# Layer one's fifth mixing product made as seven smaller ones, with the sums, gates and splits around it moved

## The chip, the core and the metric

The kernel runs on one core of a Trainium2 chip. The core has five engines with a queue of instructions each: TensorE (PE; its weight loads are shown apart as PEld), VectorE (DVE), ScalarE (ACT), GpSimd (POOL) and SyncE (SP), which here only issues DMAs. Sixteen DMA engines move the data. The metric is the device time of one execution in microseconds (us), lower is better. The result is fp32; every product is made of three matmuls of rounded parts (high by high, high by low, low by high).

## What is computed

Four residual layers over x of 2048 × 512: a linear attention block and a gated MLP that mixes along the sequence, and both once more with the same weights. A pair of the two is called a layer here ("layer one", "layer two"; `L` 0 and 1).

```python
def _A_ref(x, wqkv, wo):                 # H = 32 heads of 16
    q, k, v = qkv[0], qkv[1], qkv[2]     # of x @ wqkv
    phi = lambda t: jnp.where(t > 0, t + 1, jnp.exp(t)) + 1e-6
    pq, pk = phi(q), phi(k)
    kv = jnp.einsum("bhsd,bhse->bhde", pk, v)
    z = jnp.einsum("bhsd->bhd", pk)
    num = jnp.einsum("bhqd,bhde->bhqe", pq, kv)
    den = jnp.einsum("bhqd,bhd->bhq", pq, z)[..., None] + 1e-6
    return (num / den).transpose(...).reshape(B, S, D) @ wo

def _B_ref(x, w_in, w_sp, b_sp, w_out):  # Fh = 896
    z = _gelu(jnp.einsum("bsd,df->bsf", x, w_in))
    z1 = z[..., :Fh]
    z2 = _layernorm(z[..., Fh:], axis=-1)
    g = jnp.einsum("ts,bsf->btf", w_sp, z2) + b_sp[None, :, None]
    return jnp.einsum("bsf,fd->bsd", z1 * g, w_out)

x = A_x
x = x + _A_ref(_layernorm(x, axis=-1), A_wqkv, A_wo)
x = x + _B_ref(_layernorm(x, axis=-1), B_w_in, B_w_sp, B_b_sp, B_w_out)
x = x + _A_ref(...)                      # the same weights again
x = x + _B_ref(...)
```

The product of `w_sp` (2048 × 2048) with `z2` (2048 × 896) is the mixing, and the largest part of the work.

## The kernel before

The order of the instructions on every engine is written out by hand in Python loops; nothing reorders them. Tiles come from lists of slots that are used round robin (`pages` 22, `quads` 6, `bigs` 4, `banks` 8, the last in PSUM). A tile that takes a slot waits for the last reader of the slot's former tile.

A layer runs through three classes. `P1.run` (the first half) takes the 16 row tiles of x one after another, one step `s` each: it normalises a tile, turns it (by a store to memory, tensor `xt`, a load and a transpose on VectorE, class `Turn`), makes K and Q and adds to the product of keys and values. Up to `s` = 10 a step holds 36 matmuls, then 24, since some Q are put off. `P2.run` (the second half) finishes the attention, and makes `z` and `z1`. `P4.run` is the mixing, and behind it the output products.

The mixing is a fast matrix product: with `w_sp` and `z2` cut in halves it takes seven products instead of eight. They come in the order P2, P1, P6, P7, P4, P5, P3. A product is eight steps `g`. In a step, `fetch` loads 512 KB of weights four steps ahead, `sp` splits them two steps ahead (ScalarE the high half, VectorE the low half, lines 885 and 886) together with the matching part of z2, and `mm` issues 24 or 18 matmuls (lines 1051 to 1053). At a product's end `evac` adds the banks to the result on VectorE. A finished unit of the result is multiplied by `z1` on POOL (`gate`, line 1089), one per step from the list `gq`; POOL's queue holds the gates in the order in which they are issued, and one starts as soon as its inputs are there.

A product whose name is in `DIVIDED` is itself made as seven smaller ones: 14 steps of 12 matmuls (`mm_div`, `evac_div`, `zsum`, `zpart`). In the kernel before, these are P2 and P4 of layer two and none of layer one.

Sums of parts of `w_sp` are needed by both forms. Those of the plain seven (`Sums.tick`, 32 ticks, tensor `s`) are added on POOL, 14 ticks in `P2.run` and the rest in the mixing of layer one (`g` up to 18). Those of the divided products (`Sums.halve`, 32 parts, tensor `hP`) are made by DMAs alone: first a copy issued by SP (line 791), then an accumulating DMA issued by POOL (line 795). They run from `g` = 19 on in layer one's mixing, beside P6, P7, P4, P5 and P3, and are read in layer two.

Of the kernel before, what the change touches and what calls it, by code (L numbers as in the profile page):

```python
# [15 lines left out]
P = 128  # L16
# [35 lines left out]

DIVIDED = ((), ("P2", "P4"))


@with_exitstack
def mixer_kernel(ctx: ExitStack, tc: tile.TileContext, x_in, wqkv, wo_d, win1_d, win2_d, wsp_d, bsp_d, wout_d,
# [156 lines left out]
    class Turn:  # L214
# [3 lines left out]
        def __init__(self, name, by_pe, always=False, inbank=False):  # L218
            self.name, self.by_pe, self.always, self.inbank = name, by_pe, always, inbank
            self.held, self.d, self.raw = {}, {}, {}  # L220

# [19 lines left out]
        def get(self, i):  # L241
            if i in self.held:
                s = self.held.pop(i)
                b = transposes(s)
                if self.always:
                    pages.put(s)
                return b, banks
            r = self.raw.pop(i)
            home = banks if self.inbank else pages
            y = home.get([P, 4, P])  # L250
            nc.vector.transpose(y.rearrange("p c (t m) -> p m c t", m=4), r.rearrange("p (m c j) -> p m c j", m=4, c=4))
            pages.put(r)
            return y, home


    class P1:
# [78 lines left out]
        def K_split(self, i):  # L335
            r = self.r.pop(i)
            h, l = pages.get(PAGE, F32R), pages.get(PAGE, F32R)
            nc.scalar.activation(h, r, AF.Copy, bias=PHI_EPS)
            last = nc.vector.scalar_tensor_tensor(l, r, PHI_EPS, h.bitcast(F32), op0=OP.add, op1=OP.subtract)
# [57 lines left out]
        def start(self):  # L397
# [14 lines left out]

            def idle(n):
                for _ in range(n):
                    nc.tensor.matmul(b, ones, m, start=True, stop=True)

# [5 lines left out]
            self.T_high(0)  # L422
            idle(4)
            banks.put(b)
# [117 lines left out]
    class P2:  # L542
# [121 lines left out]
        def e2(self, i):  # L664
            z = ztag(i, [P, FH], f"z{self.L}")
            for j, b in enumerate(self.eb):
                nc.scalar.activation(z[:, j * HF:(j + 1) * HF], b, AF.Gelu_apprx_tanh)
                banks.put(b)
# [26 lines left out]
        def run(self, sums):  # L695
            w1 = self.win1
            for s in range(1, NT + 3):
# [51 lines left out]
                w1.fetch()  # L749
                if self.L == 0 and s > 4:  # L750
                    sums.tick()
                if s >= NT + 1:
# [5 lines left out]
    class Sums:  # L758
# [70 lines left out]
    class P4:  # L829
# [8 lines left out]
        def __init__(self, p2, sums):  # L838
# [10 lines left out]
            self.tmp, self.bank = {}, {}  # L849
            self.beta = self.delta = None  # L850
            self.wout = {}
# [23 lines left out]
        def sp(self, g):  # L875
            self.wsp(g)
            if g < len(self.steps) and self.steps[g][0] not in self.div:
                self.zsp(g)

# [206 lines left out]
        def gate(self, n, f):  # L1086
            z1 = self.z1.pop((n, f))
            u = self.unit(n, f)
            nc.gpsimd.tensor_tensor(u, u, z1, op=OP.mult)  # L1089
            pages.put(z1)  # L1090

        def evac(self, p):

            V, bs = nc.vector, self.bs
            gates = []
            if p in ("P1", "P5"):
                for j in range(2):
                    n = 2 + j if p == "P1" else j
                    V.tensor_add(self.unit(n, 3), self.unit(n, 3) if self.joins(p) else bs[n],  # L1099
                                 self.delta[j])  # L1100
                    gates.append((n, 3))
                banks.put(*self.delta)
            for j in range(2):
                a, b = 2 + j, j
                for f in range(3):
# [21 lines left out]
                    if p in ("P2", "P4", "P3") or (p == "P7" and "P4" in self.div):  # L1127
                        banks.put(q)
            self.gq.extend(gates)

# [21 lines left out]
        def o(self, i):  # L1152
# [10 lines left out]
            if i % 4 == 3:  # L1163
                bigs.put(self.gb[i // 4])

        def run(self, nxt):
            p2 = self.p2
            self.fetch(2)
            self.sp(0)
            if self.div:  # L1170
                self.loadb()
            ahead = deque()
            if self.div:
                self.zpart(0)
                self.zpart(1)
                ahead.extend([2, 3, 4, 5, 6, 7][:4 - 2])
                self.zsum(2)
            while p2.f():
                if ahead:
                    g = ahead.popleft()  # L1180
                    self.zsum(g + 1)
                    self.zpart(g)
            while ahead:
                g = ahead.popleft()
                self.zsum(g + 1)
                self.zpart(g)
            p2.win1.free()
# [4 lines left out]
            for g in range(n):  # L1192
                p, k = self.steps[g]
                self.fetch(g + 4)
                evac_first = p == "P6" and k == HT - 1
                div_first = p in self.div and k == 13 and p == "P4"
                if not evac_first and not div_first:
                    self.sp(g + 2)
                    self.zsum(g + 4 + 1)
                    self.zpart(g + 4)  # L1200
# [21 lines left out]
                if p == "P3":  # L1222
# [85 lines left out]
```

## Time and profile before

| | us |
|---|---|
| median of three executions | 1387.16 |
| lowest and highest | 1387.02, 1388.31 |
| the profiled execution | 1386.75 |
| its span, first to last instruction | 1384.9 |

The mean granted clock of TensorE is 1.000. Rows of the order of time read: start in us, length in us, engine, line, operation, tile written <- tiles read, sizes, count, and in brackets the idle time of that engine before it and what ended it. A suffix q on an engine means its issuing queue. Rows of a window hold its ends, its length and the busy time of PE, PEld, DVE, ACT and POOL with their instructions, then the granted clock, the DMA engines' mean share and GB/s.

### The profile page before, as it was taken

The numbers are of one execution on the slowest core, as the hardware profiler recorded it, in microseconds if no ns is written. First come the engines' busy times: TensorE is split into PE (matmuls) and PEld (weight loads), VectorE is DVE, ScalarE is ACT, GpSimd is POOL, SyncE is SP. The second block draws the span as 40 slices with busy tenths as digits, with TensorE's granted clock in tenths as the row PEclk, the third lists the DMA queues.
The fourth block names the chain that finished last, engine by engine and source line by source line (L and its number), as shares of the span: only waits on it lengthen the run. The fifth ranks groups of instructions, "written<-read, shape, count | busy, mean of one in ns | idle before, by whom it ended". The sixth has DMA issues, their size and how long they took to land.

```text
span 1384.9 us, 17460 instructions
## 1 busy us (share of the span) xinstructions
PE 1376.4 (99%) x6182; PEld 1149.0 (83%) x6182; DVE 893.1 (64%) x1331; ACT 587.6 (42%) x893; POOL 396.7 (29%) x506
## 2 busy tenths in 40 slices
PE   9999999999999999999999999999999999999998
PEld 7888888888888888878888888888888888878887
DVE  6665877752578665674566658775438667886632
ACT  6664534434323333341256646443346333633410
POOL 3333455543466201342012334432100020021300
PEclk9999999999999999999999999999999999999999
DMA  5632267775999877893735322555346445454432
GB/s 159 202 115 62 92 213 258 250 240 193 329 309 317 302 248 190 228 266 114 228 112 185 115 61 95 175 179 168 114 148 202 137 167 155 147 186 149 161 123 91
DMA packets 148344, 248.76 MB, mean 180 GB/s; under 512 B 12448, under 2 KB 51104, under 8 KB 148000
## 3 DMA queue, kind: packets, MB, share of 16 engines
q1 hardware_dynamic: 145952, 239.26, 52.2%
q0 software_dynamic: 2304, 8.39, 3.4%
q8 instruction: 48, 0.79, 0.2%
q14 instruction: 40, 0.33, 0.1%
HBM read 179.70 MB, written 84.67 MB: 191 GB/s over the span
## 4 chain that ended last, share of the span: by engine, by line
PE 91%; DVE 4%; DMA 2%; ACT 2%; issue 1%; POOL 1%; SPq 0%; ACTq 0%; DVEq 0%; POOLq 0%
PE bank L125 18%; PE bank L124 18%; PE bank L123 18%; PE bank L1052 11%; PE bank L1053 11%; PE bank L1051 11%; DMA pg<-in_wout_dram 1%; DVE qd L886 1%; PE bank L515 1%; PE bank L526 0%; ACT qd L885 0%; DVE st L186 0%; PE bank L211 0%; DMA pg<-in_wqkv_dram 0%; DVE pg L112 0%
## 5 line engine op out<-in xcount | busy, mean ns | idle before, releaser
L1052 PE MATMUL bank<-qd,pg 128*128 128x512 f32 x784 | 305.5, 390 | 1.5 <-DVE qd L886 1.5
L1053 PE MATMUL bank<-qd,pg 128*128 128x512 f32 x784 | 305.3, 389 | 0.0
L1051 PE MATMUL bank<-qd,pg 128*128 128x512 f32 x784 | 305.1, 389 | 0.0
L886 DVE TENSOR_TENSOR qd<-qd,qd 128x1024 fp32r<-128x1024 f32 x124 | 166.7, 1345 | 135.3 <-ACT qd L885 135.0
L885 ACT ACTIVATE qd<-qd 128x1024 fp32r<-128x1024 f32 x124 | 131.3, 1059 | 184.4 <-PE bank L1053 158.9
L1052 PEld LDWEIGHTS bank<-qd,pg 128*128 128x128 f32 x784 | 147.1, 188 | 33.9 <-DVE qd L886 3.5
L1053 PEld LDWEIGHTS bank<-qd,pg 128*128 128x128 f32 x784 | 147.2, 188 | 31.1 <-DVE pg L925 0.7
L1051 PEld LDWEIGHTS bank<-qd,pg 128*128 128x128 f32 x784 | 147.1, 188 | 31.0 <-ACT pg L923 0.4
L1089 POOL TENSOR_TENSOR bg<-bg,pg 128x512 f32<-128x512 f32 x56 | 83.8, 1512 | 279.6 <-DVE bg L1099 121.0
L125 PE MATMUL bank<-qd,pg 128*128 128x512 f32 x384 | 149.8, 390 | 0.1
L190 POOL TENSOR_SCALAR rs<-mv 128x1 f32<-128x1 f32 x96 | 27.3, 284 | 343.5 <-DVE mv L188 342.8
L199 ACT ACTIVATE pg<-pg,nb,rs 128x512 f32<-128x512 f32 x63 | 51.2, 812 | 172.1 <-POOL nb L193 172.0
L123 PE MATMUL bank<-qd,pg 128*128 128x512 f32 x288 | 112.4, 390 | 0.1
L124 PE MATMUL bank<-qd,pg 128*128 128x512 f32 x288 | 112.2, 390 | 0.0
L805 POOL TENSOR_TENSOR pg<-pg,pg 128x512 f32<-128x512 f32 x64 | 93.8, 1466 | 55.0 <-DMA pg<-in_wsp_dram 46.0
L123 PE MATMUL bank<-bg,qd 128*128 128x448 f32 x256 | 94.2, 368 | 0.4 <-ACT qd L109 0.4
L125 PE MATMUL bank<-bg,qd 128*128 128x448 f32 x256 | 93.6, 365 | 0.1
L124 PE MATMUL bank<-bg,qd 128*128 128x448 f32 x256 | 93.6, 366 | 0.0
L125 PE MATMUL bank<-qd,bg 128*128 128x512 f32 x224 | 87.5, 391 | 0.0
L124 PE MATMUL bank<-qd,bg 128*128 128x512 f32 x224 | 87.4, 390 | 0.0
L123 PE MATMUL bank<-qd,bg 128*128 128x512 f32 x224 | 87.2, 389 | 0.0
L123 PE MATMUL bank<-wo,qd 128*128 128x512 f32 x224 | 87.1, 389 | 0.0
(137 smaller groups left out, 2557.9 us busy)
## 6 DMA issues: line engine op xcount, KB each, us to landing
qd<-s SPq DMA_DIRECT2D x64, 512.0 KB, 3.8
qd<-in_wsp_dram SPq DMA_DIRECT2D x44, 512.0 KB, 4.2
pg<-in_wsp_dram SPq DMA_DIRECT2D x64, 256.0 KB, 4.8
s<-pg SPq DMA_DIRECT2D x64, 256.0 KB, 4.5
pg<-x SPq DMA_DIRECT2D x64, 256.0 KB, 2.9
z<-pg SPq DMA_DIRECT2D x56, 256.0 KB, 2.8
pg<-z SPq DMA_DIRECT2D x56, 256.0 KB, 4.3
x<-pg SPq DMA_DIRECT2D x48, 256.0 KB, 2.6
```

The costliest lines, as they stand in the source:

```text
L123: nc.tensor.matmul(out, ah, bh, start=start, stop=False)
L124: nc.tensor.matmul(out, ah, bl, start=False, stop=False)
L125: nc.tensor.matmul(out, al, bh, start=False, stop=stop)
L190: nc.gpsimd.tensor_scalar(rs, mv[:, 1:2], LN_EPS, None, op0=OP.add)
L199: nc.scalar.activation(y, x, AF.Identity, bias=nb, scale=rs)
L805: nc.gpsimd.tensor_tensor(t, a, b, op=OP.add)
L885: self.mark = nc.scalar.activation(w[:, 0], r, AF.Copy)
L886: nc.vector.tensor_sub(w[:, 1], r, w[:, 0].bitcast(F32))
L1051: m(out, h[:, o], w[:, 0, j, :], start=start, stop=False, skip_group_check=True)
L1052: m(out, h[:, o], w[:, 1, j, :], start=False, stop=False, skip_group_check=True)
L1053: m(out, l[:, o], w[:, 0, j, :], start=False, stop=stop, skip_group_check=True)
L1089: nc.gpsimd.tensor_tensor(u, u, z1, op=OP.mult)
```

## The change

Layer one now divides P4. The 16 parts that this product's sums take are made in layer one's mixing at `g` = 10 to 25; those of layer two's P2 are made in layer two's `P1.run`, copies at `s` = 2 to 9 and accumulations at `s` = 6 to 13. Eight ticks of the plain sums move into layer one's `P1.run` (`s` = 2 to 9), into two slots of `bigs` cut in sheets. The loads of wv and wo move from `s` = 6 to 11 and 14. The transpose of a turned tile is issued at the end of the step before. A gate waits for the newest split of weights on ScalarE (`self.mark`). `evac` takes the two delta banks last, for layer one's P1 it is issued ahead of the next split, and at the end of P7 the split for P4's third step is issued ahead of the evacuation. Four warm-up matmuls at the start are 256 columns wide instead of 512.

```diff
-DIVIDED = ((), ("P2", "P4"))
+DIVIDED = (("P4",), ("P2", "P4"))
+
+class Sheets:
+    def __init__(self, slots, n):
+        self.slots = slots
+        self.tiles = [slots.get([P, NF, 512]) for _ in range(n)]
+        self.free_list = deque(t[:, f, :] for t in self.tiles for f in range(NF))
...
@@ Turn
+            self.pre(i)
+            return self.made.pop(i)
+
+        def pre(self, i):
+            if i in self.made or i not in self.raw:
+                return
             r = self.raw.pop(i)
...
-            return y, home
+            self.made[i] = y, home
...
@@ P1.start
-            idle(4)
+            idle(4, 256)
...
@@ P1.run
-                if s == 6:
-                    self.wv, self.wo = (quads.get([P, 4, 512]) for _ in range(2))
+                if self.L == 0:
+                    if s == 2:
+                        sums.slots = Sheets(bigs, 2)
+                    if 2 <= s < 10:
+                        sums.tick(s < 9)
+                    if s == 10:
+                        sums.store()
+                        sums.slots.close()
+                        sums.slots = pages
+                elif 2 <= s < 10:
+                    sums.halve(14 + s, None)
+                if self.L == 1 and 6 <= s < 14:
+                    sums.halve(18 + s, self.mark)
+                if s == 11:
+                    self.wv = quads.get([P, 4, 512])
                     nc.sync.dma_start(self.wv, wqkv[:, 1024:1536].rearrange("(c p) f -> p c f", p=P))
+                if s == 14:
+                    self.wo = quads.get([P, 4, 512])
                     nc.sync.dma_start(self.wo, wo_d.rearrange("(c p) f -> p c f", p=P))
+                if s in range(3,NT-1):
+                    self.turn.pre(s + 1)
...
@@ Sums
-            self.parts = [(what, p, m, q) for what in ("copy", "add") for p in DIVIDED[1] for m in (1, 3, 2, 4)
+            self.parts = [(what, p, m, q) for p in ("P4", "P2") for what in ("copy", "add") for m in (1, 3, 2, 4)
                           for q in range(2)]
...
@@ P4
-            nc.gpsimd.tensor_tensor(u, u, z1, op=OP.mult)
+            behind(nc.gpsimd.tensor_tensor(u, u, z1, op=OP.mult), self.mark)
...
+        def zahead(self, g):
+            while self.zmade <= g:
+                self.zsum(self.zmade + 1)
+                self.zpart(self.zmade)
+                self.zmade += 1
...
@@ P4.run
-                evac_first = p == "P6" and k == HT - 1
+                evac_first = (p == "P6" or p == "P1" and nxt is not None) and k == HT - 1
...
                 if evac_first:
+                    if p == "P1":
+                        self.ask(3)
                     self.evac(p)
                     self.sp(g + 2)
-                if g < 19:
-                    self.sums.tick()
-                if nxt is not None:
-                    self.sums.halve(g - 19, self.mark)
+                self.sums.tick()
+                if nxt is not None and 10 <= g < 26:
+                    self.sums.halve(g - 10, self.mark)
...
+                if p == "P7" and k == HT - 1 and self.div:
+                    self.sp(g + 3)
                 if k == HT - 1 and not evac_first:
                     self.evac(p)
```

More of the change, by code (lines that the diff above doesn't have):

```diff
@@ L338, in K_split @@
             nc.scalar.activation(h, r, AF.Copy, bias=PHI_EPS)
-            last = nc.vector.scalar_tensor_tensor(l, r, PHI_EPS, h.bitcast(F32), op0=OP.add, op1=OP.subtract)
+            last = self.mark = nc.vector.scalar_tensor_tensor(l, r, PHI_EPS, h.bitcast(F32), op0=OP.add,
+                                                              op1=OP.subtract)
             self.pk[i] = (h, l)
@@ L411, in start, with idle @@
             b = banks.get(PAGE)
-            def idle(n):
+            def idle(n, w=512):
                 for _ in range(n):
-                    nc.tensor.matmul(b, ones, m, start=True, stop=True)
+                    nc.tensor.matmul(b[:, 0:w], ones, m[:, 0:w], start=True, stop=True)
             idle(10)
@@ L749, in run @@
                 w1.fetch()
-                if self.L == 0 and s > 4:
-                    sums.tick()
+                if self.L == 0:
+                    if s > 4:
+                        sums.tick()
                 if s >= NT + 1:
@@ L849, in __init__ @@
             self.tmp, self.bank = {}, {}
+            self.made = 0
             self.beta = self.delta = None
@@ L875, in sp @@
         def sp(self, g):
-            self.wsp(g)
-            if g < len(self.steps) and self.steps[g][0] not in self.div:
-                self.zsp(g)
+            while self.made < min(g + 1, len(self.steps)):
+                self.wsp(self.made)
+                if self.steps[self.made][0] not in self.div:
+                    self.zsp(self.made)
+                self.made += 1
         def wsp(self, g):
@@ L1095, in evac @@
             gates = []
[L1096 to L1102, printed above, removed]
             for j in range(2):
@@ L1128, in evac @@
                         banks.put(q)
+            if p in ("P1", "P5"):
+                for j in range(2):
+                    n = 2 + j if p == "P1" else j
+                    V.tensor_add(self.unit(n, 3), self.unit(n, 3) if self.joins(p) else bs[n],
+                                 self.delta[j])
+                    gates.append((n, 3))
+                banks.put(*self.delta)
             self.gq.extend(gates)
```

30 lines of the change are left out of this document (13 added, 17 removed).

## The prediction

> **What bounds the kernel now.** I read the page first (shares of the engines, then the chain that ended last), then TensorE's own order of time for the pitch of the matmuls, then every place where that pitch breaks, and last who was late there.
>
> ```profile
> span 1384.9 us, 17460 instructions
> PE 1376.4 (99%) x6182; PEld 1149.0 (83%) x6182; DVE 893.1 (64%) x1331; ACT 587.6 (42%) x893; POOL 396.7 (29%) x506
> PE 91%; DVE 4%; DMA 2%; ACT 2%; issue 1%; POOL 1%; SPq 0%; ACTq 0%; DVEq 0%; POOLq 0%
> ```
>
> The first line is the span, the second the busy time, the third the chain. TensorE is 91% of the chain, so a matmul taken out is time taken out, if nothing else is late. A busy time of 0.39 us is not a matmul's price, though, because they overlap. The price is the distance between starts. Here are the first matmul of layer one's fifth product (P4) and the first of its sixth (P5):
>
> ```profile
> 503.79 0.39 PE L1051 MATMUL bank<-qd,pg 128*128 128x512 f32 x1
> ...
> 547.31 0.39 PE L1051 MATMUL bank<-qd,pg 128*128 128x512 f32 x1
> ```
>
> Between them lie 8 steps of 24 matmuls: 43.52 us / 192 = 0.2267 us each, with no stall at all. The mixing of layer one breaks this pitch once, in step 6 of the last product (P3); that of layer two breaks it mainly in P4 (which is already made as seven there) and just behind:
>
> ```profile
> 615.31 0.39 PE L1051 MATMUL bank<-qd,pg 128*128 128x512 f32 x1
> 616.49 0.50 PE L1052 MATMUL bank<-qd,pg 128*128 128x512 f32 x1 [0.79 <-DVE qd L886]
> 616.96 0.50 PE L1053 MATMUL bank<-qd,pg 128*128 128x512 f32 x1
> ...
> 1188.28 0.39 PE L1051 MATMUL bank<-qd,pg 128*128 128x512 f32 x1
> ...
> 1193.72 0.39 PE L1051 MATMUL bank<-qd,pg 128*128 128x512 f32 x1
> 1194.56 0.50 PE L1052 MATMUL bank<-qd,pg 128*128 128x512 f32 x1 [0.45 <-DVE qd L886]
> ...
> 1218.95 0.39 PE L1051 MATMUL bank<-qd,pg 128*128 128x512 f32 x1
> 1219.64 0.50 PE L1052 MATMUL bank<-qd,pg 128*128 128x512 f32 x1 [0.30 <-DVE qd L886]
> ...
> 1233.87 0.39 PE L1051 MATMUL bank<-qd,pg 128*128 128x512 f32 x1
> ```
>
> From 1188.28 to 1233.87 layer two runs P4's 14 steps of 12 matmuls and the first 24 of P5: 192 matmuls in 45.59 us, so 2.07 us of stalls. About 0.75 us of it stands at 1193.72 (gaps of 0.84 and 0.34 against 0.23), the other 1.3 us from 1218.95 on. Each time the second matmul of a group waits for VectorE's low half of the weights (L886).
>
> **The change, part by part.**
>
> *The fifth product as seven.* Layer one's P4 becomes 14 steps of 12 matmuls, 168 for 192. 24 × 0.2267 = **5.44 us** leave TensorE. VectorE gets 40 more instructions, ScalarE 26, SP's queue six more loads of 512 KB. Layer two's P4 shows whether they fit:
>
> ```profile
> 1155.60:1188.30 32.70, 32.70 (x146) 27.05 (x146) 28.06 (x52) 14.03 (x21) 0.00 (x0) 1.00 0.43 131
> 1188.30:1228.00 39.70, 38.95 (x169) 31.10 (x167) 37.05 (x55) 24.53 (x37) 4.83 (x3) 1.00 0.55 172
> ```
>
> (Windows of P7 and P4: length, then busy us of PE, PEld, VectorE, ScalarE, POOL, the granted clock, the DMA share.) VectorE is busy 37 of 39.7 us: it fits, with nothing to spare. So what else touches VectorE there decides.
>
> *The P3 stall.* In step 6 of P3, ScalarE stood still for a load of w_out and the weight split behind it came late:
>
> ```profile
> 612.84 0.63 ACT L109 ACTIVATE wo<-pg 128x512 fp32r<-128x512 f32 x1 [3.30 <-DMA pg<-in_wout_dram]
> 614.46 1.97 DVE L886 TENSOR_TENSOR qd<-qd,qd 128x1024 fp32r<-128x1024 f32 x1 [0.26 <-ACT qd L885]
> ```
>
> Until 602.9 us the accumulating DMAs of the second layer's sums are issued (first row: by line, durations, first and last start). In the window of 520 to 560 us (two rows by queue: packets, MB, share of 16 engines) eight of them hold the engines for more than half the time:
>
> ```profile
> L795 POOL DMA_DIRECT2D hP<-hP x8: 805/822/837, 543.5 to 602.9; - x8
> ...
> q0 software_dynamic: 1006, 3.67, 52.0%
> q1 hardware_dynamic: 1261, 4.04, 27.0%
> ```
>
> That is 0.52 × 40 / 8 = 2.6 us of all 16 engines for each, against 0.27 × 40 / 4.04 × 0.52 = 1.4 us for a plain 512 KB. In the changed kernel no such DMA is left after the second step of P7, so w_out lands early. The gaps of 1.18 and 0.47 against 0.23 return, 1.2 us, and a little behind them: **−1.3 us** (bounds 0 and −1.3).
>
> *Gates tied to splits.* VectorE and POOL at the end of layer two's P4:
>
> ```profile
> 1213.70 3.53 POOL L1089 TENSOR_TENSOR bg<-bg,pg 128x512 f32<-128x512 f32 x2 [70.24 <-DVE bg L1017]
> ...
> 1214.14 1.95 DVE L886 TENSOR_TENSOR qd<-qd,qd 128x1024 fp32r<-128x1024 f32 x1
> 1216.01 1.84 DVE L954 TENSOR_TENSOR pg<-z_z,pg 128x256 f32<-128x256 f32 x2
> ...
> 1218.37 1.21 DVE L886 TENSOR_TENSOR qd<-qd,qd 128x1024 fp32r<-128x1024 f32 x1
> ```
>
> POOL had waited 70 us with P5's gates at the head of its queue and ran them as soon as their unit was final. Beside them L886 took 1.95 us instead of 1.21; that is the lateness at 1218.95. Tied to the split of their own step, they run in P5, whose steps have 5.44 us. So the **1.3 us** go (bounds 0 and −1.3). What queues behind a waiting gate on POOL is only the next gate, and between g = 18 and 25 an accumulating DMA read eight or more steps later.
>
> The Trainium skill's page "SBUF — State Buffer", section "Who interferes with whom", says that a VectorE instruction with two SBUF inputs and a GpSimd one that reads SBUF lock each other out for a whole instruction. The rows agree in kind (1.95 for 1.21), and it speaks against the tie: ScalarE's high half releases the gate and the low half together.
>
> A gate alone takes 1.29 us (below, 1224.33), a step of P6 needs 1.21 + 0.55 us of VectorE (L886 and L927), so even a full collision leaves it under the 4.08 us of 18 matmuls. One place is tight: P1 to P6 in layer one, where the evacuation now goes ahead of the split.
>
> ```profile
> 1224.33 1.29 POOL L1089 TENSOR_TENSOR bg<-bg,pg 128x512 f32<-128x512 f32 x1 [7.10 <-DVE bg L1017]
> ...
> 435.51 0.55 DVE L927 SCALAR_TENSOR_TENSOR pg<-z_z,pg 128x384 fp32r<-128x384 f32 x1
> 435.98 1.28 DVE L1099 TENSOR_TENSOR bg<-pg,bank 128x512 f32<-128x512 f32 x2
> 437.17 3.67 DVE L1110 TENSOR_TENSOR bg<-bg,bank 128x512 f32<-128x512 f32 x6
> ...
> 442.38 1.65 DVE L927 SCALAR_TENSOR_TENSOR pg<-z_z,pg 128x384 fp32r<-128x384 f32 x1
> 443.95 2.31 DVE L886 TENSOR_TENSOR qd<-qd,qd 128x1024 fp32r<-128x1024 f32 x1
> ...
> 442.59 0.39 PE L1051 MATMUL bank<-qd,pg 128*128 128x512 f32 x1
> ```
>
> P6's second step starts at 442.59, its first at 442.59 − 18 × 0.2267 = 438.51. The last bank is final some 0.2 us later, its evacuation (3.67 / 6 = 0.61) ends near 439.4, the two of L1099 at 440.7; L886 then ends at 441.9 and L927 at 442.4 if POOL is quiet, in time; at the slowed 2.0 and 1.65 us they end at 444.3, 1.3 us late. Bounds 0 and +1.3; one gate of 1.29 can cover only one of the two, so I take **+0.4**.
>
> *The extra split at the end of P7.* The weights for P4's third step are split ahead of the six evacuations (3.67 us by the row above) instead of behind them. At 1193.72 that removes 0.75 us in layer two. The evacuations and the copies behind them end 1.2 us later, and the fourth step's split then ends near 1196.4 against 1188.28 + 3 × 2.72 + 0.23 = 1196.67. I take **−0.7** (bounds 0 and −0.75), and for the same border in layer one **+0.2** (bounds 0 and +0.75).
>
> *Layer one's sums moved forward.* Eight of the 32 ticks go into layer one's first half (s = 2 to 9). They add about 512 KB in and 512 KB out to each step (36 matmuls, 8.16 us), 2 × 1.4 = 2.8 us of DMA, and two POOL additions ahead of the next tile's statistics (rs, nb), for which ScalarE's normalising waits. On SP's queue the stores wait for those additions and the next tile's loads stand behind them. The two 1 MB loads of wv and wo leave that stretch for s = 11 and 14. The cover is how early TensorE's operand is ready:
>
> ```profile
> 42.36 0.69 DVE L112 TENSOR_TENSOR pg<-bank,pg 128x512 fp32r<-128x512 f32 x1
> ...
> 48.30 0.39 PE L123 MATMUL bank<-qd,pg 128*128 128x512 f32 x1
> ...
> 713.00:800.00 87.00, 87.00 (x385) 72.07 (x384) 57.37 (x99) 57.68 (x98) 28.21 (x48) 1.00 0.48 146
> ```
>
> The low half ends at 43.05, the matmul that reads it is the third, at 48.76: 5.7 us. If the cover is gone, each microsecond beyond it is one of TensorE's, once per late tile. 2.8 us of DMA and 2 × 1.3 us of additions stay inside it: 0 (bounds 0 and +2). The last row is the same half of layer two: its DMA share is 0.48.
>
> *The P2 product's sums in layer two's first half.* Copies at s = 2 to 9, accumulating DMAs at s = 6 to 13. The thin place is s = 11 to 13, where a step is 24 matmuls, 5.44 us, and each tile goes through memory to be turned (xt):
>
> ```profile
> 791.63 0.37 SPq L235 DMA_DIRECT2D xt<-pg  x1
> 795.83 0.32 SPq L100 DMA_DIRECT2D pg<-xt  x1
> ...
> 798.51 0.73 DVE L251 STREAM_TRANSPOSE bank<-pg 128x512 f32<-128x512 f32 x1 [1.45 <-DMA pg<-xt]
> 799.90 0.69 DVE L112 TENSOR_TENSOR pg<-bank,z_h 128x512 fp32r<-128x512 f32 x1 [0.66 <-ACT z_h L109]
> ...
> 801.60 0.39 PE L123 MATMUL bank<-qd,z_h 128*128 128x512 f32 x1
> ```
>
> Here a slow store (4.2 us to the load behind it) made VectorE wait 1.45 us, and TensorE still had its operand 1.4 us early (800.59 to 802.05, the third matmul), so the usual cover is near 3 us. An accumulating DMA beside both store and load adds up to 2 × 2.6 = 5.2 us: 2.2 beyond the cover, in three steps 6.6. Bounds 0 and +6.6; the DMAs start only behind the store of their own step, so mostly one of the two meets them, and 2.6 stays under 3. I take **+0.8**.
>
> *Small edits at no cost.* Earlier transposes (they only move ahead of a win2 split), deltas evacuated last, the rewritten order of partial sums (same order). The halved warm-up matmuls: four of 256 columns for 512, at most 4 × 0.11 = 0.45 us; no row tells whether something else ends that stretch, so 0 with bounds ±0.45.
>
> **Sum.** −5.4 −1.3 −1.3 −0.7 + 0.4 + 0.2 + 0.8 = −7.3 us. The profiled execution took 1386.75 us, 0.41 under the median of 1387.16. So 1379.5 by that execution and **1379.9 us** as a median; I say 1380.
>
> **The rivals.**
> (a) *The matmuls go, the stalls stay and double.* VectorE sets the pace in P4 as seven, and layer one's copy shows layer two's 2.07 us. Then −5.44 − 1.3 + 2.1: 1382.5. For it: 37.05 of 39.7 us. Against it: part of those 37 is POOL's doing (1.95 for 1.21).
> (b) *Tied gates collide everywhere.* If a gate takes 1.29 us from L886 and slows L927 to 1.65, a step of P6 or P3 needs 1.21 + 1.29 + 1.65 = 4.15 us, over 4.08; over some 14 steps a layer about 1 us, both layers 2, the P1 border 0.9 more: 1383. Against it: the P6 row of 443.95 shows both slow in 3.95 us. The lock rule of the Trainium skill's page "SBUF — State Buffer" (same section), taken in full, is this case.
> (c) *The gain is given back* in layer two's first half: three late steps at 1.5 us, 1384.5 to 1387.
> (d) *Slower: the xt loop becomes the bound.* If both transfers wait behind an accumulating DMA in all eight steps s = 6 to 13, and the copies (1.4 us) take the rest of the engines, a round trip grows by 2 × (2.6 + 1.4) = 8 us against covers of 5.7 (long steps) and 3: 2.3 us in five and 5 in three, 26 us, about half because a turn spans two steps: 1380 + 13 = 1393. It decides from a growth of about 6 us. For it: 2.6 us of every engine at each step. Against it: (2.6 + 1.4) / 8.16 on top of a share of 0.48 still leaves the engines 0.97 busy, not over.
>
> **How the numbers follow.** The forecast has 0.50 (own range 1377.8, every gain at its bound, to 1383), (a) 0.15, (b) 0.10, (c) 0.12, (d) 0.13. 0.2% is 2.8 us, about what a measurement of this kernel can tell from no change: faster is under 1384.4 and holds the forecast, (a) and (b): 0.75; (c) is within it, 0.12; (d) slower, 0.13. The range runs from 1377.5 into the bottom of (d), 1389.
>
> **What would show it.** In the new trace: P4 of layer one near 38.1 us; P3 there at 32.6; no gap at 1218.95's place and gates in P5's steps; the waits of L251 for xt in layer two's first half under 3 us. I am wrong if TensorE shows gaps there, if L886 is late at P6's second step, or if the gates lengthen P3.

## The result, and the profile after

The changed kernel takes 1382.74 us (median of six executions, 1381.36 to 1383.36). The kernel before took 1387.7 us beside it (six, 1386.07 to 1388.8). The ratio is 0.9964, with a 95% interval of 0.9952 to 0.9977: faster by 5.0 us. The sum had said 7.3 us. The time lies at the upper end of the forecast's own range, where rivals (a), 1382.5, and (b), 1383, stand too, so it does not choose between them; the traces do.

The page of the changed kernel, the same three lines as were shown of before (span, busy time, chain by engine):

```profile
span 1381.2 us, 17464 instructions
...
PE 1371.3 (99%) x6158; PEld 1144.6 (83%) x6158; DVE 914.2 (66%) x1371; ACT 599.8 (43%) x919; POOL 418.6 (30%) x506
...
PE 95%; DMA 3%; DVE 1%; ACT 1%; issue 0%; SPq 0%; ACTq 0%; DVEq 0%
```

24 matmuls are gone. TensorE's share of the chain rises from 91% to 95%, VectorE's falls from 4% to 1% (its late weight splits), and the share of the DMAs rises from 2% to 3%. So the stalls that are left are of another kind: they go back to transfers, for which VectorE and ScalarE wait ahead of TensorE.

The windows of layer one's P4, P5 and P3 in the changed kernel (ends, length, busy us of PE, PEld, DVE, ACT, POOL, granted clock, DMA share, GB/s):

```profile
505.58:543.66 38.08, 38.08 (x169) 31.54 (x168) 35.59 (x57) 24.39 (x36) 0.00 (x0) 1.00 0.59 183
543.66:587.20 43.54, 43.54 (x194) 36.06 (x193) 30.94 (x39) 13.32 (x18) 13.97 (x6) 1.00 0.48 153
587.20:619.90 32.70, 32.70 (x146) 27.10 (x145) 28.67 (x29) 16.93 (x24) 17.23 (x10) 1.00 0.59 203
```

TensorE is busy for the whole of each. P4 takes 38.08 us for 43.52, which is 5.44 less, and VectorE is busy for 35.59 of them without holding anything up. No gate lies in P4 (POOL x0); they have moved into P5 and P3. P3's first and last matmul stand at 587.18 and 619.60: 32.64 us with the next start, and the stall at its sixth step is gone.

Where the rest went is seen in TensorE's order of time of the changed kernel. The first two rows are the border of P6 and P7 in layer one, the others lie in layer two's first half; in brackets the idle time and what ended it:

```profile
475.90 0.39 PE L1100 MATMUL bank<-qd,pg 128*128 128x512 f32 x1
...
476.75 0.50 PE L1098 MATMUL bank<-qd,pg 128*128 128x512 f32 x1 [0.46 <-ACT pg L970]
...
790.96 0.39 PE L143 MATMUL bank<-pg,pg 128*128 128x512 f32 x1
...
792.80 0.50 PE L141 MATMUL bank<-qd,z_h 128*128 128x512 f32 x1 [1.45 <-ACT z_h L127]
...
803.89 0.39 PE L143 MATMUL bank<-pg,pg 128*128 128x512 f32 x1
...
805.08 0.50 PE L141 MATMUL bank<-qd,z_h 128*128 128x512 f32 x1 [0.80 <-ACT z_h L127]
```

Against a pitch of 0.23 us and with the slower matmuls behind each gap, 0.9 us are lost at 476, 2.0 at 791 and 1.4 at 804. None of the three was there before. The prediction had named gaps in layer two's first half as a sign that it is wrong, and there they are.

Who was late at the last two, in the order of time of SyncE, POOL and VectorE:

```profile
781.60 0.49 SPq L511 DMA_DIRECT2D qd<-in_wqkv_dram  x1
783.96 0.33 SPq L118 DMA_DIRECT2D pg<-xt  x1
...
782.49 0.92 POOL L839 DMA_DIRECT2D hP<-hP  x1
...
787.98 0.94 POOL L839 DMA_DIRECT2D hP<-hP  x1
...
797.33 0.93 POOL L839 DMA_DIRECT2D hP<-hP  x1
...
791.38 0.73 DVE L276 STREAM_TRANSPOSE bank<-pg 128x512 f32<-128x512 f32 x1 [4.72 <-DMA pg<-xt]
...
803.67 0.73 DVE L276 STREAM_TRANSPOSE bank<-pg 128x512 f32<-128x512 f32 x1 [3.12 <-DMA pg<-xt]
```

The load of the turned tile that is issued at 783.96 is used at 791.38, 7.4 us later. Issued ahead of it are the 1 MB load of wv (781.60) and one accumulating DMA (782.49), and another (787.98) joins while it is under way. VectorE waits 4.72 us for it, then 3.12 for a later one. The prediction called a wait under 3 us the sign that this place is covered.

The account, from TensorE's starts in the two profiled executions (1386.75 and 1382.98 us):

| place | forecast | measured |
|---|---|---|
| 24 matmuls fewer | −5.44 | −5.44 |
| P3's stall, layer one | −1.3 | −1.33 |
| gates tied (end of layer two's P4, start of P5) | −1.3 | −1.2 |
| extra split at P7's end, layer two | −0.7 | −0.75 |
| the same border, layer one | +0.2 | 0 |
| P1 to P6, layer one | +0.4 | 0 |
| layer one's first half (near 48 us) | 0 | +0.8 |
| P6 to P7, layer one (476 us) | none | +0.9 |
| layer two's first half | +0.8 | +3.4 |

These add up to −3.6 us; the two executions differ by 3.8. Of the rest, a stall near 196 us that was there before costs 0.25 us more, small delays in layer two's first half 0.15 us more, the start is 0.16 us shorter and the stretch behind the last matmul 0.37 us, with which the sum is −3.75. The medians differ by 5.0 us; the 1.2 us between that and the two profiled executions lies within the spread from one execution to the next and is not accounted for.

### The profile page after: what moved, and what is told of

Its sections match the earlier page's. It is cut to its first block, busy times and chain, and to the rows that moved or that the text cites. A ratio compares the mean times of both kernels' runs of the same rounds, so it can differ in the third digit from the quotient of the medians.

```text
span 1381.2 us, 17464 instructions
## 1 busy us (share of the span) xinstructions
PE 1371.3 (99%) x6158; PEld 1144.6 (83%) x6158; DVE 914.2 (66%) x1371; ACT 599.8 (43%) x919; POOL 418.6 (30%) x506
## 4 chain that ended last, share of the span: by engine, by line
PE 95%; DMA 3%; DVE 1%; ACT 1%; issue 0%; SPq 0%; ACTq 0%; DVEq 0%
PE bank L141 19%; PE bank L143 19%; PE bank L142 19%; PE bank L1100 12%; PE bank L1099 12%; PE bank L1098 12%; DMA pg<-xt 1%; DMA qd<-s 1%; PE bank L229 1%; PE bank L558 1%; PE bank L569 0%; DMA xt<-pg 0%; PE bank L441 0%; DVE qd L933 0%; DVE bg L1153 0%
## 5 line engine op out<-in xcount | busy, mean ns | idle before, releaser
L933 DVE TENSOR_TENSOR qd<-qd,qd 128x1024 fp32r<-128x1024 f32 x130 | 166.3, 1280 | 124.2 <-ACT qd L932 123.8
L1136 POOL TENSOR_TENSOR bg<-bg,pg 128x512 f32<-128x512 f32 x56 | 104.9, 1883 | 400.3 <-ACT qd L932 330.2
L932 ACT ACTIVATE qd<-qd 128x1024 fp32r<-128x1024 f32 x130 | 137.2, 1056 | 178.0 <-PE bank L1100 121.3
L141 PE MATMUL bank<-wo,qd 128*128 128x512 f32 x224 | 87.1, 389 | 0.0
L142 PE MATMUL bank<-wo,qd 128*128 128x512 f32 x224 | 87.1, 389 | 0.0
```

The source lines that it names most:

```text
L141: nc.tensor.matmul(out, ah, bh, start=start, stop=False)
L142: nc.tensor.matmul(out, ah, bl, start=False, stop=False)
L932: self.mark = nc.scalar.activation(w[:, 0], r, AF.Copy)
L933: nc.vector.tensor_sub(w[:, 1], r, w[:, 0].bitcast(F32))
L1136: behind(nc.gpsimd.tensor_tensor(u, u, z1, op=OP.mult), self.mark)
```

## The experiments

All of these are the changed kernel with one edit, except where more is said, and none leaves out any of the work. A time of one execution moves by some 2 to 4 us from one to the next (the kernel before gave 1385.57 to 1390.10 beside these, the changed one 1381.36 to 1383.36), so for single executions the gaps in the trace decide, and times only in the two that were timed over five rounds.

**Layer two's accumulating DMAs three steps earlier.**

```diff
-                elif 2 <= s < 10:
-                    sums.halve(14 + s, None)
-                if self.L == 1 and 6 <= s < 14:
-                    sums.halve(18 + s, self.mark)
+                elif 2 <= s < 6:
+                    sums.halve(12 + 2 * s, None)
+                    sums.halve(13 + 2 * s, None)
+                if self.L == 1 and 3 <= s < 11:
+                    sums.halve(21 + s, self.mark)
```

> Layer two's accumulating DMAs move from s = 6 to 13 into s = 3 to 10, where a step has 36 matmuls (the copies go two per step into s = 2 to 5); wv stays at s = 11. My theory: the 3.4 us of gaps on TensorE in layer two's first half (791 and 804 us in the changed kernel) come from accumulating DMAs in steps of 24 matmuls, so they fall to 0.5 us or less and the span to about 1378. Rival: the 1 MB load of wv at s = 11 makes the xt load late by itself; then 1.5 us or more of gaps stay.

1377.29 us, beside 1387.77 for the kernel before; span 1375.5. Layer two's first half has no gap left (3.4 us before the edit). In this execution the gaps near 48 and 476 us, which the edit does not touch, are down to 0.2 and 0.1 us too, so its time is more than the edit's worth. The two transposes in this kernel's order of time on VectorE:

```profile
781.58 0.73 DVE L276 STREAM_TRANSPOSE bank<-pg 128x512 f32<-128x512 f32 x1 [2.48 <-DMA pg<-xt]
...
797.57 0.73 DVE L276 STREAM_TRANSPOSE bank<-pg 128x512 f32<-128x512 f32 x1 [1.71 <-DMA pg<-xt]
```

VectorE still waits for xt, but 2.48 and 1.71 us instead of 4.72 and 3.12, and that TensorE does not notice. The same eight DMAs cost nothing beside steps of 36 matmuls.

**Only the load of wv back to step 6.**

```diff
-                if s == 11:
+                if s == (11 if self.L == 0 else 6):
```

> In layer two alone wv is loaded at s = 6 again, the accumulating DMAs stay at s = 6 to 13. My theory (the accumulating DMAs): 2 us or more of the 3.4 us of gaps stay. Rival (the wv load): 1 us or less stays. If both are needed together, this one and the one with the DMAs moved each fall under 1 us.

1381.87 us, beside 1387.77; span 1380.1. The gap at 791 is gone, that at 804 stays with 1.4 us. So the first needs the 1 MB load and the accumulating DMAs together, and the second the DMAs alone. Neither theory had it whole: the share of wv is about 2 us of the 3.4, but moving the DMAs removes both.

**The dose doubled: all eight accumulating DMAs into four steps, `s` = 10 to 13.** The last three of these are short.

```diff
-                if self.L == 1 and 6 <= s < 14:
-                    sums.halve(18 + s, self.mark)
+                if self.L == 1 and 10 <= s < 14:
+                    sums.halve(4 + 2 * s, self.mark)
+                    sums.halve(5 + 2 * s, self.mark)
```

> The eight accumulating DMAs of layer two run two per step at s = 10 to 13. My theory: the gaps on TensorE in layer two's first half grow, from 3.4 us to 6 to 12 us. Rival (the wv load, or a store that is slow for another reason): they stay within 1 us of 3.4.

1394.08 us, beside 1387.77: slower than before; span 1392.3. Its order of time on POOL, VectorE and TensorE:

```profile
789.12 1.78 POOL L840 DMA_DIRECT2D hP<-hP  x2
...
794.09 0.73 DVE L276 STREAM_TRANSPOSE bank<-pg 128x512 f32<-128x512 f32 x1 [6.29 <-DMA pg<-xt]
...
807.44 0.73 DVE L276 STREAM_TRANSPOSE bank<-pg 128x512 f32<-128x512 f32 x1 [8.73 <-DMA pg<-xt]
...
790.88 0.39 PE L143 MATMUL bank<-pg,pg 128*128 128x512 f32 x1
...
795.50 0.50 PE L141 MATMUL bank<-qd,z_h 128*128 128x512 f32 x1 [4.24 <-ACT z_h L127]
...
796.23 0.63 PE L143 MATMUL bank<-qd,pg 128*128 128x512 f32 x1
796.65 0.63 PE L141 MATMUL bank<-qd,z_h 128*128 128x512 f32 x1
```

Two DMAs in a step make VectorE wait 6.3 and 8.7 us, and TensorE is idle for 4.24 and then for 5.74 us. With the slower matmuls behind each stop, layer two's first half takes 14.6 us longer than in the kernel before, above the 6 to 12 forecast. This is the mechanism of rival (d), the xt loop as the bound, and near its 1393 us; but it takes two DMAs in a step, and (d) had one. The changed kernel stands on the slope towards it. Its last two rows are taken up again at the end.

**The gates untied.**

```diff
-            behind(nc.gpsimd.tensor_tensor(u, u, z1, op=OP.mult), self.mark)
+            nc.gpsimd.tensor_tensor(u, u, z1, op=OP.mult)
```

> Gates without the tie to a split, all else as in the changed kernel. My theory: POOL runs two gates as soon as their units are final, beside VectorE's splits at the end of P4, and 1 to 1.5 us of gaps come back at the end of P4 and the start of P5 in layer two, and as many in layer one, whose P4 is now made in the same way: 2 to 3 us in all. Rival: the extra split at the end of P7 gave VectorE its room, and less than 0.5 us comes back. POOL's length of a gate falls from the 1.88 us mean towards 1.5.

1385.1 us, beside 1387.77; span 1383.3. The stalls are back, in layer one's P4 too, where the new form would have had them: 1.22 us in P4 and 0.41 in P5 in layer one, 1.31 and 0.41 in layer two. The mean length of a gate falls from 1.88 to 1.52 us, as forecast. The order of time on POOL, VectorE and TensorE without the tie:

```profile
1212.34 3.53 POOL L1136 TENSOR_TENSOR bg<-bg,pg 128x512 f32<-128x512 f32 x2 [66.20 <-DVE bg L1064]
...
1212.77 1.95 DVE L933 TENSOR_TENSOR qd<-qd,qd 128x1024 fp32r<-128x1024 f32 x1
...
1218.28 0.50 PE L1099 MATMUL bank<-qd,pg 128*128 128x512 f32 x1 [0.50 <-DVE qd L933]
```

and the same place in the changed kernel:

```profile
1212.30 1.22 DVE L933 TENSOR_TENSOR qd<-qd,qd 128x1024 fp32r<-128x1024 f32 x1
...
1229.97 2.33 POOL L1136 TENSOR_TENSOR bg<-bg,pg 128x512 f32<-128x512 f32 x1 [76.88 <-ACT qd L932]
```

The split takes 1.22 instead of 1.95 us, because the first gate now starts 17 us later, in P5. It takes 2.33 us there instead of 1.29, since the low half of its own step runs beside it: the collision is not gone, it has moved to a step with room. Of the tie's worth the prediction saw only layer two's part; the new P4 of layer one needs it just as much.

**No division in layer one, all the other edits kept.**

```diff
-DIVIDED = (("P4",), ("P2", "P4"))
+DIVIDED = ((), ("P2", "P4"))
```

> Layer one's P4 in eight steps of 24 matmuls again, everything else of the change kept (its sums are still made, for layer two). My theory: 24 matmuls more, 5.4 us on TensorE, and no gap in P4: layer one's P4 takes 43.5 us instead of 38.1, the span about 1381.2 + 5.4 = 1386.6, less up to 0.9 if the gap at P7's start goes with the extra VectorE work of P7. Rival (the seven products' VectorE work cost as much as the matmuls gave): the span grows by under 3 us.

1389.91 us, beside 1385.57; span 1388.1. P4's and P5's first matmuls:

```profile
505.61 0.39 PE L1098 MATMUL bank<-qd,pg 128*128 128x512 f32 x1
...
549.18 0.39 PE L1098 MATMUL bank<-qd,pg 128*128 128x512 f32 x1
```

43.57 us instead of 38.08: the division is worth 5.49 here, with nothing given back within the product. The span grew by 6.9 us, more than the 5.4 forecast: layer two's first half loses about 1.1 us more than in the changed kernel (its gaps are at 796.48 and 810.83 here), and the stall near 196 us and the end are 0.3 to 0.4 us longer each. The other edits alone, among them the moved sums, were no gain: this execution is 4.3 us slower than that of the kernel before beside it.

**The split for P4's third step behind P7's evacuation again.**

```diff
-                if p == "P7" and k == HT - 1 and self.div:
-                    self.sp(g + 3)
```

> The weight split for P4's third step behind P7's evacuation again. My theory: 0.5 to 0.8 us of gap at P4's third step comes back in layer two and as much in layer one, 1.0 to 1.6 us in all. Rival (the ties alone made the room): under 0.3 us.

1383.74 us, beside 1385.57; span 1382.0. The gap returns with 0.74 us in each layer; TensorE in layer two:

```profile
1192.42 0.39 PE L1098 MATMUL bank<-qd,pg 128*128 128x512 f32 x1
...
1193.26 0.50 PE L1099 MATMUL bank<-qd,pg 128*128 128x512 f32 x1 [0.45 <-DVE qd L933]
```

This is the 0.84 us step of the kernel before. The early split removes 0.75 us in layer two and as much in layer one, where the stall is one that the new form would have brought.

**Layer one's accumulating DMAs one every second step.**

```diff
-                if nxt is not None and 10 <= g < 26:
-                    self.sums.halve(g - 10, self.mark)
+                if nxt is not None and 10 <= g < 18:
+                    self.sums.halve(g - 10, None)
+                if nxt is not None and 14 <= g < 30 and g % 2 == 0:
+                    self.sums.halve(1 + g // 2, self.mark)
```

> Layer one's eight accumulating DMAs at every second step from g = 14 to 28 instead of at each of g = 18 to 25. My theory: in P6 they ask for more than a step of 4.08 us gives and make the weights' loads late (9.3 us to landing); spread, the loads land in 7 us or less and the 0.9 us of gap at P7's start falls under 0.2. Rival (VectorE's extra work in P7 and its evacuation make the gap): 0.5 us or more stays.

1381.17 us, beside 1385.57; span 1379.4. The transfers in the window of 455 to 480 us (P6's end), first in the changed kernel (queues: packets, MB, share of 16 engines; issues: count, KB each, us to landing):

```profile
q0 software_dynamic: 797, 2.87, 58.7%
...
qd<-s SPq DMA_DIRECT2D x5, 512.0 KB, 9.3
```

then with the DMAs spread:

```profile
q0 software_dynamic: 463, 1.63, 36.7%
...
qd<-s SPq DMA_DIRECT2D x6, 512.0 KB, 4.4
```

A load of weights lands in 4.4 us instead of 9.3, and the gap at P7's start is 0. The median of 9.3 does not make the gap by itself: it is 8.4 to 9.5 us in all the executions with the first placing, and some of them have no gap. What counts is one late load. The order of time on ScalarE shows it in the changed kernel:

```profile
460.00 1.06 ACT L932 ACTIVATE qd<-qd 128x1024 fp32r<-128x1024 f32 x1 [2.61 <-PE bank L1100]
...
465.82 1.06 ACT L932 ACTIVATE qd<-qd 128x1024 fp32r<-128x1024 f32 x1 [4.34 <-DMA qd<-s]
```

Two splits in P6 stand 5.82 us apart, and a step is 4.08: the second is 1.74 us late for its load. P6's evacuations and P7's first split follow on the same engines, and TensorE loses 0.9 us. The gap isn't steady, but it goes with this lateness. In the other executions with the same placing the split was late by 0, 0.1, 0.7, 1.0, 1.6, 2.0 and 2.1 us, and the gaps were 0, 0, 0, 0.2, 0.8, 1.2 and 1.2: the lateness less a cover of some 0.85 us. With the DMAs spread it was 0 in both executions. In two more (the kernel without the division and the one with P2's sums in P3) the load came in time, but the low half of the next split was slow:

```profile
465.79 4.05 DVE L929 TENSOR_TENSOR qd<-qd,qd 128x1024 fp32r<-128x1024 f32 x1 [2.39 <-ACT qd L928]
```

(the latter kernel, VectorE; L929 is L933 there.) Beside it POOL ran two gates that had been held by late loads of z1, with the issue of two DMAs, and 4.05 us stand for 1.22; the gaps were 0.6 and 0.8. What makes the loads late by so much in one execution and so little in the next is not shown.

**Layer one's ticks one step later, the loads alone ahead of them.**

```diff
-                    if 2 <= s < 10:
-                        sums.tick(s < 9)
-                    if s == 10:
+                    if s == 2:
+                        sums.fetch()
+                    if 3 <= s < 11:
+                        sums.tick(s < 10)
+                    if s == 11:
```

> Layer one's eight ticks one step later (s = 3 to 10), the first loads of w_sp at s = 2 as before, so the first additions find their operands in place. My theory: POOL's additions at s = 2 wait 3.7 us for their loads and hold the next tile's statistics behind them; ScalarE's wait of 4.1 us for nb near 35 us falls to under 1 us and the gap near 48 us (0.8 us) to under 0.2. Rival (the DMA traffic of the sums makes xt late whatever POOL does): the gap stays at 0.5 us or more.

1383.1 us, beside 1385.57; span 1381.3. In the changed kernel POOL and ScalarE show this at the first tick, and VectorE and TensorE what comes of it:

```profile
30.25 3.54 POOL L849 TENSOR_TENSOR bg<-bg 128x512 f32<-128x512 f32 x2 [3.73 <-DMA bg<-in_wsp_dram]
...
33.88 0.22 POOL L208 TENSOR_SCALAR rs<-mv 128x1 f32<-128x1 f32 x1
...
35.15 0.82 ACT L217 ACTIVATE pg<-pg,nb,rs 128x512 f32<-128x512 f32 x1 [4.14 <-POOL nb L211]
...
46.09 0.73 DVE L276 STREAM_TRANSPOSE bank<-pg 128x512 f32<-128x512 f32 x1 [1.86 <-DMA pg<-xt]
...
48.83 0.50 PE L141 MATMUL bank<-qd,pg 128*128 128x512 f32 x1 [0.42 <-DVE pg L130]
```

POOL waits 3.73 us for a transfer with the additions at the head of its queue, and the statistics of the next tile, 0.22 us of work, stand behind them. ScalarE waits 4.14 us for those. The tile is stored to xt late by it, and its load ends last: VectorE waits for it. With the ticks a step later both waits are gone, and so is the gap near 48 us (0.1 to 1.9 us in the ten executions with the first placing, 0 in both with this one). How large the gap is does not follow POOL's wait, which is 3.1 to 3.9 us in all ten, but more nearly VectorE's wait for xt: 1.49 us where the gap is smallest but one, 3.08 where it is largest. So POOL's queue uses up the cover, and the transfers beside the load set the rest. But one of 0.95 us appears at 104.9, where the load of a turned tile now meets the last ticks and the 1 MB load of wv. The time is the same.

**P2's sums back at the end of layer one's mixing.** None are made in layer two.

```diff
-                elif 2 <= s < 10:
-                    sums.halve(14 + s, None)
-                if self.L == 1 and 6 <= s < 14:
-                    sums.halve(18 + s, self.mark)
...
+                if nxt is not None and 40 <= g < 48:
+                    self.sums.halve(g - 24, None)
+                if nxt is not None and 50 <= g < 58:
+                    self.sums.halve(g - 26, self.mark)
```

> The sums of layer two's P2 made at the end of layer one's mixing instead of in layer two's first half: copies at g = 40 to 47, accumulating DMAs at g = 50 to 57, so four of them beside P3's first steps. My theory of the gap that P3 had before (accumulating DMAs make w_out late, ScalarE waits, the next split is late): 0.8 us or more of gap comes back in P3, and the 3.4 us in layer two's first half go. Rival (the traffic of z1, x and the weights, or POOL's gates, made that gap): P3 stays under 0.3 us.

1383.32 us, beside 1386.66; span 1381.5. Layer two's first half has no gap, and P3 has its stall again, 2.1 us, with 0.65 us more just behind it (627.9 us), which was not followed. The transfers from 585 to 612 us, in the changed kernel and then in this one:

```profile
pg<-in_wout_dram SPq DMA_DIRECT2D x7, 256.0 KB, 4.5
```

```profile
q0 software_dynamic: 641, 2.36, 49.7%
...
pg<-in_wout_dram SPq DMA_DIRECT2D x7, 256.0 KB, 7.8
```

The same DMAs at this place make w_out land in 7.8 us instead of 4.5, and the order of time shows ScalarE behind it and TensorE behind VectorE:

```profile
610.58 0.63 ACT L127 ACTIVATE wo<-pg 128x512 fp32r<-128x512 f32 x1 [4.17 <-DMA pg<-in_wout_dram]
...
615.01 0.50 PE L1096 MATMUL bank<-qd,pg 128*128 128x512 f32 x1 [1.05 <-DVE pg L968]
```

So the cause that the prediction gave for P3's stall is shown by putting it back. Eight accumulating DMAs have to go somewhere: beside P5 and P3 they cost 2 to 2.7 us, in the short steps of layer two 3.4, and in the long steps nothing.

**The early DMAs timed, and all the repairs together.** The first is the kernel of the first experiment again, over five rounds:

> The kernel with only layer two's accumulating DMAs moved to s = 3 to 10, timed. My theory: 3.4 us under the changed kernel, 1379 to 1380, and 1 to 2 us over the one with all three edits. If the one look at 1377.3 is typical, the other two edits are worth nothing that a time can tell.

The second has that edit, the spread DMAs and the later ticks in one, and loads wv and wo three and one steps later:

```diff
-                if s == 11:
+                if s == 14:
                     self.wv = quads.get([P, 4, 512])
...
-                if s == 14:
+                if s == 15:
                     self.wo = quads.get([P, 4, 512])
```

> Three edits together: layer two's accumulating DMAs in s = 3 to 10 (copies two per step), layer one's at every second step from g = 14 to 28, layer one's ticks one step later; and wv and wo at s = 14 and 15 in both layers, behind the last xt load. My theory: each of the gaps of the changed kernel goes for its own cause, 3.4 us in layer two's first half, 0.9 at P7, 0.8 near 48 us and the 0.95 us that the later ticks brought at 105 us beside wv; a span near 1375.5 and a median near 1377. If the causes share one wait that only moves on (late loads that turn up elsewhere), the median stays at 1379 or above.

| | median us | lowest, highest | ratio to before, 95% |
|---|---|---|---|
| early DMAs alone | 1378.52 | 1378.02, 1380.14 | 0.9935, 0.9922 to 0.9947 |
| all together | 1377.80 | 1377.08, 1380.46 | 0.9934, 0.9920 to 0.9947 |

Both beat the kernel before (1387.68, nine executions) by some 9 us, and the changed kernel (0.9964) by 4 to 5: the intervals of the ratios do not meet. Between the two there is no difference that can be told; the 1 to 2 us forecast between them are not seen. With all of them the span is 1375.4 us, and of the stalls only the one near 196 us (0.8 us) and 0.27 us in layer two's P2 are left.

## Why the prediction was right, and where its sum was off

The forecast, faster through the 24 matmuls with the transfers mostly covered, is what happened, and its own range (1377.8 to 1383) holds the time, at its upper end. The four negative terms came out within 0.1 us each. What made the gain 5.0 instead of 7.3 us are the terms for the moved sums, and one of the prediction's own signs of being wrong, gaps in layer two's first half, came true.

- *The fifth product as seven*: right, 5.44 us by the trace and 5.49 by taking the division out. Rival (a), stalls that double, was right about what the bare division would do: without the tie, layer one's P4 and P5 lose 1.6 us, and without the early split 0.74. It fell because the tie and the early split also work there.
- *The P3 stall*: right, with its cause. The price of a DMA there was a little low: the row of L795 that the prediction shows holds starts from 543.5 to 602.9 us, not the eight issued between 520 and 560, and in that window 3.67 MB moved, which is seven times 512 KB. So it is 0.52 × 40 / 7 = 3.0 us each instead of 2.6. Where no accumulating DMA is left w_out lands in 4.5 us; with them back it takes 7.8 and the stall is there.
- *Gates tied to splits*: right. Rival (b), collisions that delay every step, fell: gates and splits do slow each other down in P5, P6 and P3, but those steps have room. One place is left to it, the last steps of P6 in two executions (4.05 us for a split, 0.6 and 0.8 us of TensorE). The rule of the Trainium skill's page "SBUF — State Buffer", section "Who interferes with whom", that a VectorE instruction with two SBUF inputs and a GpSimd one that reads SBUF block each other, agrees in kind with the rows (2.33 us for a gate of 1.29). In P5 that time is not on the path.
- *P1 to P6* was over-priced at +0.4. The changed kernel's VectorE and POOL there:

```profile
440.21 1.28 DVE L1172 TENSOR_TENSOR bg<-pg,bank 128x512 f32<-128x512 f32 x2
441.40 1.22 DVE L933 TENSOR_TENSOR qd<-qd,qd 128x1024 fp32r<-128x1024 f32 x1
442.54 0.55 DVE L974 SCALAR_TENSOR_TENSOR pg<-z_z,pg 128x384 fp32r<-128x384 f32 x1
...
443.80 3.90 POOL L1136 TENSOR_TENSOR bg<-bg,pg 128x512 f32<-128x512 f32 x2 [5.48 <-ACT qd L932]
```

The split and the copy ran at their quiet 1.22 and 0.55 us, since the two gates came only afterwards, at 443.80. They end at 443.1 for the 442.4 worked out, and everything here stands 0.9 us later than before (505.58 for 503.79 at P4's start, less the 0.9 at P7's). TensorE shows no gap.

- *Layer one's sums in its first half*: 0 was said, with a bound of +2; it was +0.8. The step that failed is "2.8 us of DMA and 2 × 1.3 us of additions stay inside" the cover of 5.7 us: it left out the 3.73 us in which POOL waits for the transfer ahead of the additions, with the next tile's statistics queued behind. The queue behind the waiting instruction is what the prediction named and did not add up. The late store and load of xt that follow from it took up the rest of the cover.
- *P6 to P7 in layer one*: not in the sum at all. The prediction said of the DMAs moved to `g` = 10 to 25 only that none is left later, which lets w_out land early; what they do where they now stand was not priced. Beside P6 they hold 58.7% of the engines (52% beside P4 and P5 before), P6's steps are 4.08 us instead of 5.44, and its loads of 512 KB landed in 9.3 us. A forecast by that row would have had a term here.
- *The xt loop in layer two's first half*: +0.8 was said, with bounds 0 and +6.6; it was +3.4, the largest miss. The cover near 3 us was about right: a wait of 3.12 costs 0.8 us of idling and one of 4.72 costs 1.45, so it was 2.3 and 3.3. The step that failed is "mostly one of the two meets them, and 2.6 stays under 3": at 3.0 us for a DMA nothing is left of the cover, and one load met two accumulating DMAs and the 1 MB load of wv, which the prediction had listed as leaving for `s` = 11 but not counted there.

Rival (c) had this place right, but expected three late steps and the whole gain gone; there were two, and they took 3.4 of the 8.7 us that the four gains brought. Rival (d) is real but needs twice the DMAs in a step.

Left open: why the loads beside P6 are later in some executions than in others, and the stall near 196 us, where ScalarE waits some 8 us for POOL in the kernel before and after it and which no run here touched.

## What to carry to other kernels

When transfers are moved away from a stall, price them at the place where they land as carefully as at the one that they leave: which loads stand beside them, how far ahead these are issued, and what else (here a 1 MB weight load) has been moved into the same steps. Work whose deadline is far off belongs beside the longest steps, and that is worth trying first: the same eight DMAs cost 3.4 us, 2 us or more, or nothing by their place alone. A small instruction in an in-order queue is as late as the transfer that the instruction ahead of it waits for, so count the wait and not only the work.

## What the runs showed of the hardware

- *The granted clock after a long stop.* With the doubled dose two matmuls start at 790.88 and 795.50 us, with 4.24 us of idling between them, and the matmuls behind it were 0.427 us apart instead of 0.227 for some 3.4 us (796.23 and 796.65 above). The windows of that kernel there:

```profile
795.50:799.00 3.50, 3.50 (x9) 2.48 (x10) 2.65 (x5) 2.93 (x5) 1.25 (x4) 0.64 1.00 200
800.00:802.00 2.00, 2.00 (x10) 1.67 (x9) 0.00 (x0) 0.00 (x0) 1.80 (x3) 1.00 0.48 34
```

The granted clock is 0.64 in the first and 1.00 again in the second. The stop of 5.74 us that follows shows the same. One of 2.87 us (starts at 796.48 and 799.73 in the kernel without the division) was not followed by this. So the stop of 4.24 us cost some 1.6 us more than its length: eight pitches, 0.2 us longer each. The Trainium skill's page "TensorE: Matmul & The Clock Gate", section "Part 1: The HAM clock gate", says that the clock is halved after an idle window of about 3.4 us and comes back after as long a time of work. The trace agrees: the half rate came after 4.24 us of idling, not after 2.87, and lasted 3.4 us.

- *Short gaps cost more than their length too.* At a granted clock of 1.00 the matmuls behind a gap were slower too: three of them 0.34, 0.39 and 0.34 us apart in layer two's first half, one of 0.34 us near 48 us and in P4. That is 0.1 to 0.4 us on top, and it goes with the place and not with the length of the gap.
- *An accumulating DMA of 512 KB takes the time of about two plain ones* (3.0 us of all 16 engines between 520 and 560 us in the kernel before and 2.7 between 455 and 480 in the changed one, for 1.4), and plain loads beside a row of them landed in 9.3 instead of 4.4 us (weights) and 7.8 instead of 4.5 (w_out).
